# Turning one half batch of q, k and x with crossbar transposes instead of TensorE transposes, and splitting the last output tile, in a fused attention and squared-ReLU kernel

## The chip, the cores and the metric

The kernel runs on one core of a Trainium2 chip. The metric is device time in microseconds (us) per execution; a verdict compares fast runs only, with a 95% interval, and calls a difference real beyond 2%. PE is TensorE, DVE VectorE, ACT ScalarE, POOL GpSimd, SP SyncE; a name with q behind it is that engine's sequencer.

## The reference, cut to what matters

```python
# q, k, v: (4, 8, 768, 64) float32; n_global = 8, n_local = 96
scores = scale * np.matmul(q, k.transpose(0, 1, 3, 2)) + bias     # bias: minus slope of the head x distance
scores = np.where(is_global | is_local, scores, -1e9)             # local window and first 8 keys
a = softmax(scores)
x = np.matmul(a, v)            # -> 3072 tokens x 512
h = np.maximum(x @ w_in, 0.0)  # w_in 512 x 2048
out = (h * h) @ w_out          # w_out 2048 x 512, float32 out
```

The window reaches back less than 128 positions, so each tile of 128 queries needs only its own tile of keys, the one before it, and the 8 global keys.

## The kernel before

The eight "half batches" (384 tokens each, numbered 0 to 7) go through a software pipeline: while TensorE does the two dense layers of one half, it does the attention of the next half in between. To multiply q by k, both must lie with the head dimension on partitions, and the attention result x must be turned too. There are two ways to turn a tile: a TensorE transpose into PSUM followed by a copy, or a DMA "crossbar" transpose from SBUF to SBUF on SP's queue. In the kernel before, halves 0 to 2 use TensorE and halves 3 to 7 the crossbar.

```python
stage_p = ctx.enter_context(tc.tile_pool(name="stage", bufs=2))   # sq, sk: float16 q and k as loaded
...
def list_loads(x):                       # GpSimd's queue: loads that cast float32 to float16
    before = (prev.turned if prev else []) + (halves[x.hb - 1].turned if x.hb > 3 else [])
    ...                                  # plan.load(0.85, emit, before), three each for q, k, v
def turn(x, a):                          # pair a of heads: 6 TensorE transposes into PSUM, 2 copies
    ...
        nc.tensor.transpose(out=trp[:, i, t, :], in_=st[:, t, 2 * a:2 * a + 2, :], identity=ident)
def turn_by_dma(x):                      # one transfer for q and one for k of the half
    ...
        nc.sync.dma_start_transpose(out=x.bt.qk[:, 1 - i, ts]..., in_=getattr(x, name)...)
    for a in range(NPAIR):               # fix_k: DVE copies part of k into kb
        x.qk_ops[a] = x.turned + [plan.add(*fix_k(x, a), x.turned[:1], wait=4.0)]
def to_x(x, a): ...                      # 3 TensorE transposes and a copy
def to_x_by_dma(x, a):
    ...
        nc.sync.dma_start_transpose(out=x.xt[:, a, :]..., in_=st["tm"]...)
...
def attention(x):
    early = x.hb > 2
    for a in range(NPAIR):
        at = 0.04 + 0.16 * a if early else 0.1 + 0.17 * a
        jobs.append((at, lambda a=a: score(x, a)))
        jobs.append((at + 0.17, lambda a=a: attend(x, a)))
        if early:
            jobs.append((at + 0.17, lambda a=a: to_x_by_dma(x, a)))
        else:
            jobs.append((0.04 * a, lambda a=a: turn(x, a)))
            jobs.append((at + 0.3, lambda a=a: to_x(x, a)))
```

Two things matter later. A planner in Python, with estimated durations, chooses the order in which each engine gets its instructions. On the chip an engine can then stand at an instruction whose data is late although others behind it could run (the early loads below show VectorE doing so for 13.92 us). And `stage_p` has two buffers per name, so the loads of half 3 go into the buffers of half 1 and wait on the chip only for half 1, whatever the planner's `before` list says.

The softmax here doesn't subtract the row's maximum and nothing guards it: scores larger than these inputs give would overflow.

Of the kernel before, what the change touches and what calls it, by code (L numbers as in the profile page):

```python
# [8 lines left out]
FP32 = mybir.dt.float32  # L9
# [4 lines left out]
P = 128  # L14
# [130 lines left out]
def kernel(  # L145
# [11 lines left out]
    nc = tc.nc  # L157
# [3 lines left out]
    d_model, d_ff = moe_w_in.shape  # L161
    NT = S // P
    NPAIR = H // 2
    NFT = d_ff // P
    NCT = d_model // P
    HALF = S // 2
    HT = HALF // P
    NHB = 2 * B
# [17 lines left out]
    plan = Plan(1.0, 24.0)  # L186
# [5 lines left out]
    def copy(e, out, in_):  # L192
        if e == "ACT":
            nc.scalar.copy(out=out, in_=in_)  # L194
        else:
            eng(e).tensor_copy(out=out, in_=in_)
# [94 lines left out]
    def list_loads(x):  # L291
        r0 = x.half * HALF
        prev = halves[x.hb - 2] if x.hb >= 2 else None
        before = (prev.turned if prev else []) + (halves[x.hb - 1].turned if x.hb > 3 else [])
        vbefore = [halves[x.hb - x.half - 3].attended[-1]] if x.hb >= 4 else []

        def rows(src, name, t):
            def emit(e):
                dst = (x.bt.v[:, x.half * HT + t, :, 0:D] if name == "v"
                       else staged(x, name)[:, t, :, :])  # L300
                nc.gpsimd.dma_start(out=dst, in_=src[x.b, :, r0 + t * P:r0 + (t + 1) * P, :]  # L301
                                    .rearrange("h p d -> p h d"))
            return plan.load(0.85, emit, vbefore if name == "v" else before)

        if x.half == 0:
            def start(e):
                new_batch(x.bt)
                nc.vector.memset(x.bt.v[:, :, :, D:D + 1], 1.0)
            x.bt.op = plan.add({"DVE": 0.1}, start, vbefore, rank=0)
        if x.hb > 1:  # L310
            x.q_in = [rows(q, "sq", t) for t in range(HT)]
            x.k_in = [rows(k, "sk", t) for t in range(HT)]
            x.v_in = [rows(v, "v", t) for t in range(HT)]
        elif x.hb == 1:
            x.k_in, x.q_in, x.v_in = zip(*((rows(k, "sk", t), rows(q, "sq", t), rows(v, "v", t))
                                           for t in range(HT)))
        else:
            def first(dst, src, eng, e, lag):
                raw = stage_p.tile([P, H, D], FP32, name="r" + dst, tag="r" + dst, bufs=1)
                op = plan.add({e: 0.5}, lambda e: eng.dma_start(  # L320
                    out=raw, in_=src[0, :, 0:P, :].rearrange("h p d -> p h d")), rank=-1)
                op.lag = lag

                def emit(e):
                    copy(e, staged(x, dst)[:, 0], raw)
                return plan.add({"DVE": 0.42, "ACT": 0.54}, emit, [op], rank=0)
            x.k_in = [first("sk", k, nc.scalar, "ACT", 4.1)]
            x.q_in = [first("sq", q, nc.sync, "SP", 3.4)]
            x.v_in = []
            for t in range(1, HT):  # L330
                x.k_in.append(rows(k, "sk", t))
                x.q_in.append(rows(q, "sq", t))
                x.v_in.append(rows(v, "v", t - 1))
            x.v_in.append(rows(v, "v", HT - 1))
        for l in x.v_in:
            l.needs.append(x.bt.op)
        x.bt.v_in = [*getattr(x.bt, "v_in", []), *x.v_in]
# [18 lines left out]
    def fix_v(bt, t0, t1):  # L356
        def emit(e):
            copy(e, bt.vb[:, t0 - 1:t1 - 1], bt.v[:, t0:t1])
            copy(e, bt.vb[0:GR, t0 - 1:t1 - 1], bt.v[0:GR, 0:1].to_broadcast(
                [GR, t1 - t0, H, D + 1]))  # L360
        op = plan.add({"DVE": 0.85}, emit, [bt.v_in[0], *bt.v_in[t0:t1]],
                      wait=0.0 if bt is batches[0] else 4.0)
        for t in range(t0, t1):
            bt.vb_ops[t] = op

    def fix_k(x, a):
        t0, t1 = tiles_before(x)

        def emit(e):
            kt = x.bt.qk[:, 1, :, a, :]  # L370
            copy(e, x.bt.kb[:, a, t0 - 1:t1 - 1, GR:P], kt[:, t0:t1, GR:P])
            copy(e, x.bt.kb[:, a, t0 - 1:t1 - 1, 0:GR],
                 kt[:, 0:1, 0:GR].to_broadcast([P, t1 - t0, GR]))
        return {"DVE": 0.2 + 0.08 * (t1 - t0)}, emit

    def turn(x, a):
        state = {}

        def emit(e):
            state["ps"] = trp = ps_att.tile([P, 2, HT, P], FP16, name="trp", tag="att")  # L380
            warm(trp.rearrange("p i t c -> p (i t c)"))
            for i, st in enumerate((x.sq, x.sk)):
                for t in range(HT):
                    nc.tensor.transpose(out=trp[:, i, t, :], in_=st[:, t, 2 * a:2 * a + 2, :],  # L384
                                        identity=ident)
        job = plan.pe(6 * 0.056, emit, x.q_in + x.k_in + [ident_op], [att])

        def evac(i):
            def emit(e):
                copy(e, x.bt.qk[:, i, x.half * HT:(x.half + 1) * HT, a, :], state["ps"][:, i])  # L390
            return plan.after(job, {"ACT": 0.39, "DVE": 0.31}, emit)
        ops = [evac(0), evac(1)]
        x.turned.append(job)
        x.qk_ops[a] = ops + [plan.add(*fix_k(x, a), [ops[1]])]


    def turn_by_dma(x):
        ts = slice(x.half * HT, (x.half + 1) * HT)
        late = list(halves[x.hb - 2].x_ops.values()) if x.hb > 3 else []
        for i, (name, loads) in enumerate((("sk", x.k_in), ("sq", x.q_in))):  # L400
            def emit(e, i=i, name=name):
                nc.sync.dma_start_transpose(
                    out=x.bt.qk[:, 1 - i, ts].rearrange("p t a c -> p (t a) c"),
                    in_=getattr(x, name).rearrange("p t h d -> p (t h d)"))
            op = plan.add({"SP": 1.7}, emit, [*loads, x.bt.op, *late])
            op.lag = 2.5
            x.turned.append(op)
        for a in range(NPAIR):
            x.qk_ops[a] = x.turned + [plan.add(*fix_k(x, a), x.turned[:1], wait=4.0)]

    GROUPS = {
        0: ([(0, 0), (1, 0), (1, 1)], [(2, 0), (2, 1)]),
# [106 lines left out]
    def to_x_by_dma(x, a):  # L519
        st, norm = x.tm[a]  # L520

        def emit(e):
            if x.xt is None:
                x.xt = h_p.tile([P, NCT, HALF], FP16, name="xt", tag="xt")
            nc.sync.dma_start_transpose(
                out=x.xt[:, a, :].rearrange("p (t c) -> p t c", c=P),
                in_=st["tm"].rearrange("p t e d -> p (t e d)"))
        x.x_ops[a] = plan.add({"SP": 1.2}, emit, [norm])
        x.x_ops[a].lag = 2.5
# [56 lines left out]
    def layer2(x, j, m0):  # L586
# [15 lines left out]
        if m0 + 4 == NFT:  # L602
            def evac(e):
# [4 lines left out]
            plan.add({"SP": 0.6}, lambda e: nc.sync.dma_start(out=out[r0:r0 + P, :], in_=st["y"]),  # L608
                     [y_op])

    for x in halves:
        x.turned, x.attended = [], []
        x.qk_ops, x.phat, x.tm, x.x_ops, x.h2_ops, x.l1, x.l2 = {}, {}, {}, {}, {}, {}, {}
        x.xt = x.h2 = None
# [120 lines left out]

    def attention(x):
        jobs = []
        early = x.hb > 2
        for a in range(NPAIR):
            at = 0.04 + 0.16 * a if early else 0.1 + 0.17 * a  # L740
            jobs.append((at, lambda a=a: score(x, a)))
            jobs.append((at + 0.17, lambda a=a: attend(x, a)))
            if early:
                jobs.append((at + 0.17, lambda a=a: to_x_by_dma(x, a)))
            else:
                jobs.append((0.04 * a, lambda a=a: turn(x, a)))
                jobs.append((at + 0.3, lambda a=a: to_x(x, a)))
        return sorted(jobs, key=lambda j: j[0])

    def merge(main, side):  # L750
# [7 lines left out]
    def l1(x, m0=0):  # L758
        return [lambda m=m: layer1(x, [m]) for m in range(m0, NFT)]

    def l2(x):
        return [lambda j=j, m0=m0: layer2(x, j, m0) for j in range(HT) for m0 in range(0, NFT, 4)]
# [21 lines left out]
    jobs = {}  # L784
# [18 lines left out]
        job()  # L803
    for hb in range(1, NHB):
        x = halves[hb]
        for y in halves[2:4] if hb == 1 else halves[hb + 2:hb + 3]:
            list_loads(y)
        if hb == 1:
            fix_v(halves[2].bt, 1, 2)
        main = l2(x0)[6:] + l2(x) if hb == 1 else l1(x) + l2(x)  # L810
        side = attention(halves[hb + 1]) if hb + 1 < NHB else []
        merge(main, side)
        if hb + 2 < NHB:
            t0, t1 = tiles_before(halves[hb + 2])
            for t in range(t0, t1):
                fix_v(halves[hb + 2].bt, t, t + 1)
            turn_by_dma(halves[hb + 2])
# [37 lines left out]
```

## Time and profile before

| | before |
|---|---|
| time, three runs at first | 222.17 us median (221.47 to 222.4) |
| first trace | 1217.1 us, in a run of 1218.93 us: TensorE was busy for 1211.9 us in it, more than five times as long as in the later trace |
| a later trace at full speed | span 223.6 us, in a slow run: 225.36 us, over 1.5% above the fastest (221.22) of its 20 neighbours (median 222.12) |
| TensorE busy in the later trace | 212.5 us, 95% |

The prediction had only the first trace and shows its lines below. What it could not show is this, from the page of the later trace of the same kernel, taken after the prediction: the clock that TensorE was granted and the load of the DMA engines, in tenths, in 40 slices of 5.6 us.

```profile
span 223.6 us, 4828 instructions
PEclk9999999999999999996999999999999999999999
DMA  9999999999999999999799721157012101220012
```

For the first 23 slices, until about 129 us, the DMA engines are nearly always busy; after that they are mostly idle. This row decides the case. (An ordinary run, that of the tail-only kernel below, shows the same 23 slices.) In the first trace the same bytes were spread over 1217 us (slices of 30 us), so most transfers in it met idle engines:

```profile
DMA  9909000056005002700001000100000000000000
```

And in the later trace TensorE began half 2's first scores, which the changed kernel makes wait, without any idle time before them:

```profile
55.72 0.40 PE L434 MATMUL sp<-qk 64*128 64x128 f16 x8
```

### The profile page before, as it was taken

What the parts mean: (1) busy time and instruction counts of PE and PEld (TensorE: products, weight loads), DVE (VectorE), ACT (ScalarE), POOL (GpSimd) and SP (SyncE); (2) the same over time, 40 slices, a digit from 0 to 9 for tenths busy, and PEclk for the clock granted to TensorE, in tenths of its full rate; (3) what the DMA queues carried; (4) which work ended last, traced back from release to release, by engine and by line L of the source; (5) the groups of instructions that cost most, each with busy time, mean ns of one, the idle gap of its engine ahead of it and who ended that gap; (6) DMA issues with size and microseconds to landing.
All of it is one profiled execution on the core that took longest, in us unless ns stands there. A gap on an engine that the chain in (4) does not pass through costs nothing.

```text
span 1217.1 us, 4828 instructions
## 1 busy us (share of the span) xinstructions
PE 1211.9 (100%) x1912; PEld 457.0 (38%) x1912; DVE 119.1 (10%) x336; ACT 136.9 (11%) x288; POOL 68.6 (6%) x84
## 2 busy tenths in 40 slices
PE   9999999999999999999999999999999999999998
PEld 8765665233333342233322333233322333223322
DVE  2111110001010110001100111001100111000000
ACT  2121101001101110011000110011100211001100
POOL 6203000012001000200000000000000000000000
DMA  9909000056005002700001000100000000000000
GB/s 161 103 0 65 0 1 0 1 56 47 9 22 47 4 6 25 73 9 7 3 12 43 4 3 7 43 9 3 7 12 9 9 6 4 12 17 0 1 9 17
DMA packets 106583, 26.41 MB, mean 22 GB/s; under 512 B 99392, under 2 KB 103488, under 8 KB 106560
## 3 DMA queue, kind: packets, MB, share of 16 engines
q0 software_dynamic: 77024, 13.37, 14.0%
q1 hardware_dynamic: 28496, 12.46, 4.1%
q10 hardware_dynamic: 1040, 0.26, 0.1%
q8 instruction: 15, 0.25, 0.1%
q14 instruction: 8, 0.07, 0.0%
HBM read 27.26 MB, written 6.29 MB: 28 GB/s over the span
## 4 chain that ended last, share of the span: by engine, by line
PE 100%; ACT 0%; DVE 0%; POOL 0%; issue 0%; POOLq 0%
PE yps L593 42%; PE hps L544 42%; PE av L489 4%; PE sp L434 4%; PE trp L210 2%; PE trp L628 1%; PE sp L661 1%; PE av L700 1%; PE sp L654 1%; PE trx L727 1%; PE trp L384 1%; PE sp L207 1%; PE trx L513 0%; PE av L207 0%; PE hps L207 0%; ACT y L194 0%
## 5 line engine op out<-in xcount | busy, mean ns | idle before, releaser
L544 PE MATMUL hps<-xt,w_in_sb 128*128 128x384 f16 (+2 forms) x608 | 517.6, 1215 | 0.0
L593 PE MATMUL yps<-w_out_sb,h 128*128 128x512 f16 x384 | 514.2, 1701 | 0.0
L544 PEld LDWEIGHTS <-w_in_sb 128*128 128x128 f16 x608 | 187.4, 316 | 288.7 <-issue 284.6
L593 PEld LDWEIGHTS <-h 128*128 128x128 f16 x384 | 120.1, 315 | 351.3 <-issue 350.7
L568 ACT ACTIVATE hr<-hps 128x384 f16<-128x384 f32 (+1 forms) x108 | 54.9, 508 | 449.1 <-PE hps L544 422.1
L579 DVE TENSOR_TENSOR h<-hr 128x768 f16<-128x768 f16 (+1 forms) x70 | 36.6, 524 | 566.3 <-ACT hr L568 565.8
L194 ACT COPY y<-yps 128x512 f32<-128x512 f32 x24 | 14.0, 585 | 466.6 <-PE yps L593 466.6
L489 PEld LDWEIGHTS <-phat 128*128 128x128 f16 x264 | 41.7, 220 | 24.5 <-issue 23.1
L489 PE MATMUL av<-v,phat 128*128 128x65 f16 x168 | 44.7, 445 | 0.0
L449 ACT ACTIVATE ex<-sp 128x384 f16<-128x384 f32 x96 | 39.3, 464 | 40.0 <-PE sp L434 38.4
L489 PE MATMUL av<-vb,phat 128*128 128x65 f16 x96 | 36.3, 460 | 0.0
L301 POOL DMA_DIRECT2D sq<-in_q_dram x23 | 20.6, 904 | 219.3 <-DMA qk<-sq 125.9
L434 PE MATMUL sp<-qk 64*128 64x128 f16 x168 | 30.2, 612 | 0.0
L301 POOL DMA_DIRECT2D sk<-in_k_dram x23 | 20.7, 920 | 134.7 <-DMA qk<-sk 133.5
L434 PEld LDWEIGHTS <-qk 64*128 64x128 f16 x168 | 12.3, 175 | 41.4 <-issue 41.2
L301 POOL DMA_DIRECT2D v<-in_v_dram x24 | 21.6, 927 | 90.5 <-DVE rec L496 90.5
L496 DVE RECIPROCAL rec<-av 128x6 f32<-128x6 f32 x24 | 4.7, 196 | 219.0 <-PE av L489 219.0
L434 PE MATMUL sp<-qk,kb 64*128 64x128 f16 x96 | 25.4, 724 | 0.0
L210 PE MATMUL trp<-ident,zero 128*128 128x128 f16 x58 | 20.1, 710 | 1.7 <-DVE ident L233 1.7
L210 PEld LDWEIGHTS <-zero 128*128 128x128 f16 x58 | 16.6, 313 | 3.7 <-DVE zero L769 1.2
L700 PEld LDWEIGHTS <-ph 128*128 128x128 f16 x88 | 15.2, 234 | 3.2 <-issue 2.5
L434 PEld LDWEIGHTS <-kb 64*128 64x128 f16 x96 | 15.8, 329 | 1.3
(65 smaller groups left out, 289.6 us busy)
## 6 DMA issues: line engine op xcount, KB each, us to landing
out_dram<-y SPq DMA_DIRECT2D x24, 256.0 KB, 2.0
v<-in_v_dram POOLq DMA_DIRECT2D x24, 128.0 KB, 4.7
sk<-in_k_dram POOLq DMA_DIRECT2D x23, 128.0 KB, 4.5
sq<-in_q_dram POOLq DMA_DIRECT2D x23, 128.0 KB, 4.3
w_in_sb<-in_moe_w_in_dram POOLq DMA_DIRECT2D x4, 512.0 KB, 8.6
w_out_sb<-in_moe_w_out_dram POOLq DMA_DIRECT2D x4, 512.0 KB, 13.6
xt<-tm SPq DMA_TRANSPOSE x20, 2.3
rsk<-in_k_dram ACTq DMA_DIRECT2D x1, 256.0 KB, 4.7
```

What stands on the lines that cost most here:

```text
L194: nc.scalar.copy(out=out, in_=in_)
L207: nc.tensor.matmul(ps[:, 0:n], lhsT=zero[:, 0:P], rhs=zero[:, 0:n], start=True, stop=True)
L210: nc.tensor.transpose(out=ps[:, 0:n], in_=zero[:, 0:P], identity=ident)
L301: nc.gpsimd.dma_start(out=dst, in_=src[x.b, :, r0 + t * P:r0 + (t + 1) * P, :] .rearrange("h p d -> p h d"))
L434: nc.tensor.matmul(pair[h][:, i * P:(i + 1) * P], lhsT=lhsT, rhs=bt.qk[rows, 0, r, a, :], start=True, stop=True)
L449: nc.scalar.activation(out=st["ex", g][:, h, 0:n], in_=st[g][h][:, 0:n], func=AF.Exp, scale=scale)
L489: nc.tensor.matmul(av[:, h, j, :], lhsT=phat[:, h, c * P:(c + 1) * P], rhs=rhs, start=n == 0, stop=n == len(mine) - 1)
L544: nc.tensor.matmul(st["ps"][:, i * n:(i + 1) * n], lhsT=w_in_sb[:, kk, m * P:(m + 1) * P], rhs=x.xt[:, kk, c0:c1], start=kk == 0, stop=kk ...
L568: nc.scalar.activation(out=o, in_=i, func=AF.Relu)
L579: eng(e).tensor_tensor(out=x.h2[:, m0:m0 + width, c0:c1], in0=hr, in1=hr, op=ALU.mult)
L593: nc.tensor.matmul(st["ps"], lhsT=x.h2[:, m, j * P:(j + 1) * P], rhs=w_out_sb[:, m, :], start=m == 0, stop=m == NFT - 1)
L700: nc.tensor.matmul(av[:, a - a0, h, :], lhsT=st["ph", before][:, h, a, :], rhs=rhs, start=not before, stop=before == kinds[-1])
```

## The change

Its intent: TensorE bounds the kernel, so take 36 transposes of half 2 from it (24 of q and k, 12 of x) and give them to the DMA crossbar; list the loads of half 3 after half 2's transposes; and write the last output tile in two column halves, so that the first is copied and sent under the matmuls of the second.

```diff
-        before = (prev.turned if prev else []) + (halves[x.hb - 1].turned if x.hb > 3 else [])
+        before = (prev.turned if prev else []) + (halves[x.hb - 1].turned if x.hb > 2 else [])
 ... (fix_v, turn_by_dma: shorter waits in the planner for half 2)
+    def last_layer2(x, j):        # the last tile: two groups of 16 matmuls of 256 columns,
+        ...                       # each with its own copy and its own output transfer
     def attention(x):
-        early = x.hb > 2
-            at = 0.04 + 0.16 * a if early else 0.1 + 0.17 * a
+            at = 0.04 + 0.16 * a if x.hb > 2 else 0.05 + 0.14 * a
-            if early:
-                jobs.append((at + 0.17, lambda a=a: to_x_by_dma(x, a)))
-            else:
-                jobs.append((0.04 * a, lambda a=a: turn(x, a)))
-                jobs.append((at + 0.3, lambda a=a: to_x(x, a)))
+            jobs.append((at + 0.17, lambda a=a: to_x_by_dma(x, a)))
 ...
-        for y in halves[2:4] if hb == 1 else halves[hb + 2:hb + 3]:
+        if hb == 1:
+            list_loads(halves[2])
+            turn_by_dma(halves[2])
+            fix_v(halves[2].bt, 1, 2)
+        for y in halves[hb + 2:hb + 3]:
             list_loads(y)
+        if hb == NHB - 1:
+            main = main[:-NFT // 4] + [lambda: last_layer2(x, HT - 1)]
```

More of the change, by code (lines that the diff above doesn't have):

```diff
@@ L361, in fix_v @@
         op = plan.add({"DVE": 0.85}, emit, [bt.v_in[0], *bt.v_in[t0:t1]],
-                      wait=0.0 if bt is batches[0] else 4.0)
+                      wait=0.0 if bt is batches[0] else 0.5 if t1 == 2 and bt is batches[1] else 4.0)
         for t in range(t0, t1):
@@ L404, in emit @@
                     in_=getattr(x, name).rearrange("p t h d -> p (t h d)"))
-            op = plan.add({"SP": 1.7}, emit, [*loads, x.bt.op, *late])
+            op = plan.add({"SP": 1.7}, emit, [*loads, x.bt.op, *late], wait=4.0 if x.hb == 3 else 0.0)
             op.lag = 2.5
@@ L408, in turn_by_dma @@
         for a in range(NPAIR):
-            x.qk_ops[a] = x.turned + [plan.add(*fix_k(x, a), x.turned[:1], wait=4.0)]
+            x.qk_ops[a] = x.turned + [plan.add(*fix_k(x, a), x.turned[:1],
+                                                 wait=4.0 if x.hb > 2 else 0.5)]
     GROUPS = {
@@ L609, in layer2, with emit, evac @@
                      [y_op])
+    def last_layer2(x, j):
+        n = d_model // 2
+        r0 = x.hb * HALF + j * P
+        for c in range(0, d_model, n):
+            st = {}
+            def emit(e, c=c, st=st):
+                st["ps"] = ps_big.tile([P, 512], FP32, name="yps", tag="big")
+                for m in range(NFT):
+                    nc.tensor.matmul(st["ps"][:, 0:n], lhsT=x.h2[:, m, j * P:(j + 1) * P],
+                                     rhs=w_out_sb[:, m, c:c + n], start=m == 0, stop=m == NFT - 1)
+            def evac(e, st=st):
+                st["y"] = y_p.tile([P, d_model], FP32, name="y", tag="y")
+                copy(e, st["y"][:, 0:n], st["ps"][:, 0:n])
+            job = plan.pe(NFT * (n / 2400 + 0.003), emit, [x.h2_ops[m, j] for m in range(NFT)], [big])
+            y_op = plan.after(job, {"ACT": 0.3, "DVE": 0.35}, evac)
+            plan.add({"SP": 0.6}, lambda e, c=c, st=st: nc.sync.dma_start(
+                out=out[r0:r0 + P, c:c + n], in_=st["y"][:, 0:n]), [y_op])
     for x in halves:
@@ L805 @@
         x = halves[hb]
-        for y in halves[2:4] if hb == 1 else halves[hb + 2:hb + 3]:
+        if hb == 1:
[3 more added lines that the diff above has]
+        for y in halves[hb + 2:hb + 3]:
             list_loads(y)
-        if hb == 1:
-            fix_v(halves[2].bt, 1, 2)
         main = l2(x0)[6:] + l2(x) if hb == 1 else l1(x) + l2(x)
+        if hb == NHB - 1:
+            main = main[:-NFT // 4] + [lambda: last_layer2(x, HT - 1)]
         side = attention(halves[hb + 1]) if hb + 1 < NHB else []
```

## The prediction

> **What bounds the kernel now.** I read the times first, then the head of the page, the groups of instructions split by form, the data transfers, three stretches at the start, and the timeline of the last ten microseconds. From the head of the page:
>
> ```profile
> span 1217.1 us, 4828 instructions
> PE 1211.9 (100%) x1912; PEld 457.0 (38%) x1912; DVE 119.1 (10%) x336; ACT 136.9 (11%) x288; POOL 68.6 (6%) x84
> GB/s 161 103 0 65 0 1 0 1 56 47 9 22 47 4 6 25 73 9 7 3 12 43 4 3 7 43 9 3 7 12 9 9 6 4 12 17 0 1 9 17
> PE 100%; ACT 0%; DVE 0%; POOL 0%; issue 0%; POOLq 0%
> ```
>
> The span contradicts the times: three runs took 221.47 to 222.4 us, the profiled one 1217.1. TensorE is busy for 1211.9 us, more than five whole executions. So this trace shows a TensorE far slower than in the timed runs, and every wait of TensorE is hidden in it. The reader should take from it the counts and shapes of TensorE's instructions and the durations of everything else, but no TensorE duration and no absence of a wait. The groups by form:
>
> ```profile
> L593 PE MATMUL yps<-w_out_sb,h 128*128 128x512 f16 x384 | 514.2, 1701 | 0.0
> L544 PE MATMUL hps<-xt,w_in_sb 128*128 128x384 f16 x416 | 419.8, 1372 | 0.0
> ...
> L194 ACT COPY y<-yps 128x512 f32<-128x512 f32 x24 | 14.0, 585 | 466.6 <-PE yps L593 466.6
> ...
> L449 ACT ACTIVATE ex<-sp 128x256 f16<-128x256 f32 x24 | 9.3, 388 | 2.0 <-PE sp L434 0.3
> ...
> L384 PE MATMUL trp<-ident,sq 128*128 128x128 f16 x12 | 5.6, 719 | 0.0
> L384 PE MATMUL trp<-ident,sk 128*128 128x128 f16 x12 | 5.5, 704 | 0.0
> L513 PE MATMUL trx<-ident,tm 128*128 128x128 f16 x12 | 5.4, 675 | 0.0
> ```
>
> The two dense layers are 384 x 512 + 416 x 384 + 96 x 256 + 96 x 128 = 393,216 columns. At one column per cycle of the skill's 2.4 GHz plus 2.5 ns for each of the 992 matmuls that is 166 us. The same rule gives the other 920 matmuls 35 us (the 264 + 88 scores, on half the array's rows, at 0.55 of the rule because two can run side by side: my choice). The stream is about 201 us of the 222: in the timed runs, too, TensorE bounds the kernel, with some 21 us of start, end and waits. Vector and scalar work (119 and 137 us) fits beneath it. What shortens TensorE's stream, the opening or the tail shortens the run; nothing else does.
>
> **What the skill says.** (1) Perfetto Trace Analysis, section "Identifying the Most-Contended Engine": matmul busy time is no measure of the distance to the limit, because matmuls are pipelined. The trace agrees: 100% busy at 5.5 times the timed duration. (2) TensorE: Matmul & The Clock Gate, "Back-to-back issue gap": N/2.4 + 2.5 ns for a warm matmul of N columns, 56 ns for 128 columns, but about 81 ns in a stream of weight load and matmul pairs of 128 columns. The trace's 719 and 1701 ns cannot confirm either; the run's 222 us is compatible with 201 us of stream. (3) DMA: Bandwidth & Descriptors, "Rules for kernel authors": transfers issued from different engines run on the same 16 DMA engines and interleave. So crossbar transposes share them with the loads around them; no run here shows by how much. (4) Same page, "Anatomy of one DMA": a fixed cost of about 2.0 us per transfer, mostly waiting for completion. The trace agrees: 256 KB of output lands in 2.0 us.
>
> **The change part by part.** *Half batch 2.* Removed from TensorE: the 24 transposes of q and k (L384) and the 12 of x (L513). 36 x 56 ns = 2.0 us; at the 81 ns of paired streams 2.9 us; by share of busy time, (5.6 + 5.5 + 5.4) / 1211.9 x 222.17 = 3.0 us. I take 2.3, near the lower value, because the other matmuls around them hide part of a weight load. All of it lies on the path, as TensorE has no slack. The 8 + 4 copies out of PSUM go too (0.48 us each on ACT, 0.36 on DVE, some 5 us), but off the path: worth 0 by themselves. Added: two crossbar transposes for q and k and four for x, on SP's queue.
>
> ```profile
> out_dram<-y SPq DMA_DIRECT2D x24, 256.0 KB, 2.0
> ...
> xt<-tm SPq DMA_TRANSPOSE x20, 2.3
> ...
> qk<-sq SPq DMA_TRANSPOSE x5, 3.9
> qk<-sk SPq DMA_TRANSPOSE x5, 3.9
> ```
>
> They cost TensorE nothing unless it reaches its scores before they land. The program's order shows that TensorE's stream is the same up to the point where half 2's first transposes stood, after 24 output matmuls. In the changed kernel half 2's first scores follow 4 output matmuls later, at 43.6 us of the stream (by the rule above). When are q and k turned?
>
> ```profile
> 0.00:10.00 10.00, 8.33 (x27) 7.50 (x28) 4.54 (x17) 5.07 (x13) 9.25 (x16) 1.00 1.55 135
> 10.00:40.00 30.00, 30.00 (x101) 23.58 (x99) 2.74 (x10) 5.25 (x10) 14.23 (x18) 1.00 1.54 182
> ...
> 5.44 0.43 DVE L196 CAST sk<-rsk 128x512 f16<-128x512 f32 x1
> ```
>
> The first two rows are stretches; their last column is GB/s, 135 in the first 10 us and 182 from 10 to 40. The third is a line of the timeline: start, duration, instruction. Ahead of half 2's q and k stand 6.8 MB as the trace counts them (16 loads of 131 KB, two of 262, eight weight loads of 524). They need 10 + (6.82 - 1.35) / 0.182 = 40 us; the six loads, 0.79 MB, 4.3 more: 44.4. Plus 3.9 for the transpose and about 0.35 for the first copy of k: 48.6 us. TensorE's stream can't do its first real transposes before 5.9 us (end of the second cast above), where the rule puts them at 2.0; so it reaches the scores at 43.6 + 3.9 = 47.5 us without any later wait. But 222.17 - 201 - 3.9 leaves 17 us; some 1.8 lie outside the span (1218.93 for the run against 1217.1) and 3 in the tail, so 12 us are waits and small-tile losses. Most should be in the opening, where short tiles chain from engine to engine; with half of them there TensorE arrives at 53 us, 5 us after the data. I put 0.5 us on the chance of a wait and on new PSUM waits, since the scores, which take four of six banks each, now come slightly closer together (2.5 instead of 3.1 jobs apart).
>
> *The loads of half 3 behind them.* On GpSimd's queue the order of loads is unchanged, and they wait for no crossbar transpose of half 2: the new dependency only steers the planner. So it costs nothing, but these 1.2 MB can meet half 2's transposes.
>
> *Last tile in two column halves.* Today, after the last matmul:
>
> ```profile
> 1207.79 5.81 PE L593 MATMUL yps<-w_out_sb,h 128*128 128x512 f16 x4
> ...
> 1213.64 0.58 ACT L194 COPY y<-yps 128x512 f32<-128x512 f32 x1 [20.58 <-PE yps L593]
> 1214.25 0.33 SPq L608 DMA_DIRECT2D out_dram<-y  x1
> ```
>
> Afterwards the first half is copied and written under the second half's 16 matmuls. What remains is a copy of 256 columns, 388 ns by the ACT row of that width instead of 585: 0.2 us. The transfer is 128 KB instead of 256; most of its 2.0 us is fixed, so I take 0.3 off. Sixteen more matmuls cost 16 x 2.5 ns = 0.04. Sum: 0.45 us gained.
>
> Total: -2.3 - 0.45 + 0.5 = -2.25 us, or 219.9 from 222.17 (1.0%).
>
> **The rivals.** *The turn takes the gain back.* TensorE stalls at half 2's first scores because the transposes land late. For it: 47.5 against 48.6 us above if the opening has no waits, and loads of v and of half 3 running beside them. If the transposes take twice 3.9 us, the scores wait up to 4 us longer. Against it: the 12 us of waits not accounted for. It would give 221 to 224. *The gain is larger.* The transposes stood in a chain (transpose, copy out, copy of k, scores) through two PSUM buffers; if TensorE waited there, up to 2 us more go: 217 to 218. The trace cannot speak for it, since the slow TensorE hides such waits; against it, 1.2 us of output matmuls stand between neighbouring links. *SP's queue holds back x.* The crossbar transposes of x for pairs 1 and 2 stand behind half 3's transpose of k, which waits for its loads. Those follow half 2's loads directly and land by about 52 us; x is wanted when 60.7 us of stream are done. Against it, then; if it happens, 1 to 3 us are lost.
>
> **Range and chances.** Removed work between 2.0 and 3.0, tail 0.2 to 0.7, new waits 0 to 2: the change lies between -3.7 and -0.2, and the runs before spread by 0.9 us. So 218.4 to 221.9. Over 2% faster means below 217.7, which needs an unseen chain to go: 6%. Over 2% slower means above 226.6, a stall beyond anything estimated: 3%. Within 2%: 91%.
>
> **What would show it.** Right: 1892 matmuls in TensorE's row (36 fewer, 16 more), no transposes of half 2 left in the groups, six crossbar transposes each of q and of k and 24 of x among the transfers; at the end a copy near 0.39 us in place of 0.58. A stall would show as idle time of TensorE before half 2's first scores, ended by a transfer or by DVE's copy of k, or before half 2's first layer, ended by a transpose of x; if the trace is of a slow TensorE again, it can show neither, and the landing times of half 2's transposes must serve. I would be wrong if these land far above 3.9 us and the time is 222 or more, or if the time is below 217.7: then TensorE waited for something that this trace hides.

## The result, and the profile after

| | before | changed |
|---|---|---|
| median | 222.28 us (221.47 to 222.55, 4 runs) | 232.06 us (229.17 to 233.67, 4 runs) |
| ratio of fast runs | | 1.0368 [1.0268, 1.0467]: slower |

Ratios here and below are the mean time of one kernel's fast runs over that of the other's fast runs of the same rounds, so they are not quite the ratio of the medians. Two of the changed kernel's four runs (233.67 and 232.65 us) were labelled slow, being over 1.5% above its fastest. The profiled run was the fastest, 229.17 us.

The page of the changed kernel, at full speed this time, to be held against the rows above:

```profile
span 227.4 us, 4799 instructions
...
PE 211.7 (93%) x1892; PEld 126.3 (56%) x1892; DVE 116.6 (51%) x333; ACT 123.9 (54%) x280; POOL 68.5 (30%) x84
...
PEclk9999999999589999999999999999999999999999
DMA  9999999999999999999799660129011200211012
...
PE 67%; DMA 25%; POOL 5%; DVE 1%; issue 1%; ACT 0%; SPq 0%; POOLq 0%
```

There are 1892 matmuls, as intended. But TensorE is busy for 93% of a longer span, its clock falls in slices 11 and 12 (57 to 68 us), and DMA has 25% of the chain that ended last (the last row). The timeline of TensorE shows where; the columns are start, duration, instruction, and in brackets the idle time before it with what ended it:

```profile
52.81 0.38 PE L594 MATMUL yps<-w_out_sb,h 128*128 128x512 f16 x1
59.55 0.61 PE L435 MATMUL sp<-qk 64*128 64x128 f16 x8 [6.36 <-DMA qk<-sk]
60.20 4.92 PE L594 MATMUL yps<-w_out_sb,h 128*128 128x512 f16 x12
...
81.26 0.32 PE L545 MATMUL hps<-xt,w_in_sb 128*128 128x384 f16 x1 [1.04 <-DMA xt<-tm]
82.71 0.97 PE L545 MATMUL hps<-xt,w_in_sb 128*128 128x384 f16 x5 [1.13 <-DMA xt<-tm]
```

TensorE is done with its other work at 52.81 + 0.38 = 53.2 us and then stands for 6.36 us, until the transpose of half 2's k has landed. The next twelve matmuls of 512 columns take 4.92 us, where twelve take 2.76 at full clock (below). A second pair of waits, 2.2 us in all, comes before half 2's first dense layer, for the transposed x. Stretches of 2 us of the same trace; the third figure from the end is the granted clock:

```profile
54.00:56.00 2.00, 0.00 (x0) 0.00 (x0) 0.00 (x0) 0.00 (x0) 0.87 (x1) 1.00 1.71 67
...
60.00:62.00 2.00, 2.00 (x11) 0.70 (x6) 0.84 (x7) 1.43 (x4) 0.97 (x2) 0.50 2.41 158
...
64.00:66.00 2.00, 2.00 (x26) 1.03 (x25) 0.05 (x1) 0.57 (x2) 1.79 (x4) 0.85 2.42 158
```

The clock is halved towards the end of the wait and comes back only about 5 us after work resumes. Last, the transfers issued from 40 to 50 us, with size and median time from issue to landing, and then the issue of the two transposes on SP's queue:

```profile
sq<-in_q_dram POOLq DMA_DIRECT2D x3, 128.0 KB, 10.6
sk<-in_k_dram POOLq DMA_DIRECT2D x3, 128.0 KB, 13.9
qk<-sq SPq DMA_TRANSPOSE x1, 10.4
qk<-sk SPq DMA_TRANSPOSE x1, 13.2
```

```profile
43.66 2.34 SPq L402 DMA_TRANSPOSE qk<-sq  x1
46.33 5.03 SPq L402 DMA_TRANSPOSE qk<-sk  x1
```

The transpose of k, issued at 46.33, lands 13.2 us later, at 59.5; that ends the wait. Beside it run half 3's loads of q, k and v, which GpSimd issued between 43.1 and 51.6 us.

How large is the loss as a sum? The tail-only kernel below has the old turns and a trace of an ordinary run (222.31 us, span 220.5, one wait of 1.05 us for x). Against it the changed kernel has 6.36 + 2.17 - 1.05 = 7.5 us more waiting and 4.92 - 2.76 + 0.61 - 0.40 = 2.4 us at half clock, and 36 transposes less (2.0 us): 7.9. The spans differ by 227.4 - 220.5 = 6.9, so the three items account for the loss to within about a microsecond. (The openings differ too: the tail-only trace has one wait of 2.4 us there, the changed kernel's several short ones.) The other runs of the changed kernel are 2.3 to 4.5 us longer; the turn-only trace below shows such a run, with longer waits of the same two kinds.

### The profile page after: what moved, and what is told of

The parts are those of the page before. It is cut to its first block, busy times and chain, and to the rows that moved or that the text cites. A ratio compares the mean times of both kernels' runs of the same rounds, so it can differ in the third digit from the quotient of the medians.

```text
span 227.4 us, 4799 instructions
## 1 busy us (share of the span) xinstructions
PE 211.7 (93%) x1892; PEld 126.3 (56%) x1892; DVE 116.6 (51%) x333; ACT 123.9 (54%) x280; POOL 68.5 (30%) x84
## 3 DMA queue, kind: packets, MB, share of 16 engines
q0 software_dynamic: 77024, 13.37, 83.2%
## 4 chain that ended last, share of the span: by engine, by line
PE 67%; DMA 25%; POOL 5%; DVE 1%; issue 1%; ACT 0%; SPq 0%; POOLq 0%
PE yps L594 29%; PE hps L545 28%; DMA qk<-sk 8%; DMA w_out_sb<-in_moe_w_out_dram 6%; DMA sk<-in_k_dram 5%; PE sp L435 4%; DMA w_in_sb<-in_moe_w_in_dram 4%; PE av L490 4%; DMA xt<-tm 2%; POOL v L301 2%; PE yps L622 2%; POOL sq L301 1%; POOL w_in_sb L342 1%; POOL sk L301 1%; DVE phat L462 0%
## 5 line engine op out<-in xcount | busy, mean ns | idle before, releaser
L545 PE MATMUL hps<-xt,w_in_sb 128*128 128x384 f16 (+2 forms) x608 | 89.6, 301 | 2.9 <-DMA xt<-tm 2.2
L594 PE MATMUL yps<-w_out_sb,h 128*128 128x512 f16 x368 | 84.5, 386 | 0.0
L545 PEld LDWEIGHTS <-w_in_sb 128*128 128x128 f16 x608 | 53.7, 98 | 30.0 <-issue 2.6
L594 PEld LDWEIGHTS <-h 128*128 128x128 f16 x368 | 35.8, 99 | 42.0 <-issue 3.0
L194 ACT COPY y<-yps 128x512 f32<-128x512 f32 (+1 forms) x24 | 13.6, 567 | 63.7 <-PE yps L594 61.2
L435 PE MATMUL sp<-qk 64*128 64x128 f16 x168 | 9.1, 223 | 6.4 <-DMA qk<-sk 6.4
L499 DVE TENSOR_TENSOR tm<-av,rec 128x384 f16<-128x384 f32 x24 | 13.4, 557 | 0.9
L497 DVE RECIPROCAL rec<-av 128x6 f32<-128x6 f32 x24 | 4.7, 197 | 15.6 <-PE av L490 15.3
L490 PEld LDWEIGHTS <-phat 128*128 128x128 f16 x264 | 9.9, 98 | 3.4
L490 PE MATMUL av<-v,phat 128*128 128x65 f16 x168 | 11.4, 194 | 0.0
L490 PE MATMUL av<-vb,phat 128*128 128x65 f16 x96 | 10.2, 194 | 0.0
```

What stands on the lines that cost most here:

```text
L194: nc.scalar.copy(out=out, in_=in_)
L435: nc.tensor.matmul(pair[h][:, i * P:(i + 1) * P], lhsT=lhsT, rhs=bt.qk[rows, 0, r, a, :], start=True, stop=True)
L490: nc.tensor.matmul(av[:, h, j, :], lhsT=phat[:, h, c * P:(c + 1) * P], rhs=rhs, start=n == 0, stop=n == len(mine) - 1)
L499: nc.vector.tensor_tensor(out=st["tm"].rearrange("p t e d -> p e t d"), in0=av[:, :, :, 0:D], in1=rec[:, :, :, None].to_broadcast([P, 2, H ...
L545: nc.tensor.matmul(st["ps"][:, i * n:(i + 1) * n], lhsT=w_in_sb[:, kk, m * P:(m + 1) * P], rhs=x.xt[:, kk, c0:c1], start=kk == 0, stop=kk ...
L594: nc.tensor.matmul(st["ps"], lhsT=x.h2[:, m, j * P:(j + 1) * P], rhs=w_out_sb[:, m, :], start=m == 0, stop=m == NFT - 1)
```

## The experiments

Theory A, formed from these traces: in the first 130 us the DMA engines are saturated, a crossbar transpose shares them with the casting loads, and so it lands late; TensorE, which now depends on it, waits and then loses its clock. Rival B: these transposes are slow by themselves, loads or not. Rival C (the recorded expectations call it H): they are late because SP's queue issues in order, and what stands ahead of them takes time.

All fourteen kernels were correct. "Before" in each set is the kernel before, run on the same chip in the same rounds.

### The kernel before again, at full speed

No edit; a look.

> The kernel before, unchanged, for a trace at TensorE's full speed, which the first trace of it was not. Both theories: about 222.2 us. Theory A (the crossbar transposes of half 2 were stretched by the loads of half 3 that are in flight with them): half 3's crossbar transposes of q and k are slow here too, since half 4's loads flow beside them, but they are not awaited: TensorE idles under 0.5 us between 45 and 85 us and its clock stays at 1.0 there. Rival B (a crossbar transpose of q or k simply takes over 10 us at this place, whatever runs beside it): the same here, it can't be told apart by this run.

One run, 225.36 us (recorded as state unknown, a slow run by its neighbours). Its trace gave the rows shown under "Time and profile before". It also has the disease in a small form: half 3's q and k, turned by the crossbar among the loads, took 6.6 and 5.7 us to land, but had 20 us to do so; half 3's x did not, and TensorE waited 2.61 us for it at about 100 us, after which its clock was halved for a few microseconds (in the tail-only trace, an ordinary run, the wait is 1.05 us and the clock stays). The experiment on half 3's x below shows these lines.

### The two parts apart: tail only, and turn only

```diff
 # tail only: the kernel before, plus last_layer2 and
+        if hb == NHB - 1:
+            main = main[:-NFT // 4] + [lambda: last_layer2(x, HT - 1)]
 # turn only: the changed kernel, without these two lines
```

> The kernel before with the last output tile in two column halves and nothing else. The prediction's term: 0.45 us less than before, a ratio of 0.998. If the tail costs something (more matmuls, two transfers instead of one): 1.000 or more. Neither A nor B bears on it.

> The changed kernel with the last output tile in one piece: half 2's crossbar transposes alone. A and B both: the whole loss is here, about 9 to 10 us over before (ratio 1.035 to 1.05), with TensorE idle some 6 us before half 2's first scores, at half clock for some 5 us after it, and idle 2 us more before half 2's first layer. If the tail were part of the loss, the ratio would be under 1.03.

Tail only: 222.10 us (220.42 to 223.36, 14 runs), ratio 0.9996 [0.997, 1.0023]. Turn only: 233.62 us (233.52 to 234.55, 4 runs), ratio 1.0516 [1.0465, 1.0567]. So the turn is the whole loss. The tail's copy fell from 0.59 to 0.37 us and its transfer from 2.0 to 1.7, as predicted, but a gain of 0.45 us (0.2%) is inside the interval and stays unresolved. The turn-only trace has the waits of the changed kernel, longer: 7.22 us for k, then 1.99 and 1.36 us for x.

### Each half of the turn alone: q and k, and x

```diff
 # q and k alone: the changed kernel, half 2's x back on TensorE
-            jobs.append((at + 0.17, lambda a=a: to_x_by_dma(x, a)))
+            if x.hb > 2: jobs.append((at + 0.17, lambda a=a: to_x_by_dma(x, a)))
+            else:        jobs.append((at + 0.3, lambda a=a: to_x(x, a)))
 # x alone: the kernel before, half 2's x by crossbar
-                jobs.append((at + 0.3, lambda a=a: to_x(x, a)))
+                jobs.append((at + 0.17, lambda a=a: to_x_by_dma(x, a)))
```

> The changed kernel with half 2's x turned on TensorE again: the crossbar turns its q and k alone, half 3's loads not gated. A: the first wait (6 to 8 us, and half clock for some 5 us after it) is all there, the second wait is gone; 227.5 to 230.5 us, that is 2 us or more less than the 231 to 233 of the whole change. If q and k were not the main cost: under 225.

> The kernel before with half 2's x turned by the crossbar, q and k on TensorE as before: removes 12 transposes from TensorE (0.7 us by 56 ns each). A: the four transposes of x share the DMA engines with half 3's crossbar transposes and half 4's loads, land in 7 to 10 us instead of 2.3, and TensorE waits for the last of them before half 2's first layer by 0 to 4 us: 221.5 to 226. H: x stands before half 3's transposes on SP's queue here (the program's order shows it), so no wait at all: 221 to 222.

q and k alone: 228.27 us (226.73 to 229.71), ratio 1.0267 [1.0199, 1.0335]. x alone: 226.96 us (226.66 to 228.65), ratio 1.0235 [1.0169, 1.0301]. Four runs each; both intervals reach just under 2%, so both verdicts are "unclear" at that line, but both are clearly above 1. Together, 2.7 + 2.4 = 5.1%, they add up to the 5.2% of the turn-only kernel, within their intervals. The time of x alone is just above the range that theory A expected, and far above the 221 to 222 us of the rival. With q and k alone TensorE waits 6.26 us at the scores, as in the changed kernel. With x alone, the summary of the x tiles and a line of TensorE's timeline:

```profile
DMA to landing us min/median/max: 3.5/7.0/7.6
```

```profile
77.83 1.06 PE L544 MATMUL hps<-xt,w_in_sb 128*128 128x384 f16 x5 [3.19 <-DMA xt<-tm]
```

The transposes of x land in 7.0 us (median) here. Each was issued within 0.1 us of the end of its producer on DVE (the last at 70.94, after 70.91), so nothing was held back on SP's queue. So rival C is not needed for a wait: slow landing alone makes one. But in the changed kernel C is at work too: x's last pair was ready at 75.5 us and issued at 78.31, behind half 3's k and the other x transposes. The end of its producer on DVE, and two issues on SP's queue:

```profile
74.98 0.56 DVE L499 TENSOR_TENSOR tm<-av,rec 128x384 f16<-128x384 f32 x1
```

```profile
72.48 2.35 SPq L402 DMA_TRANSPOSE qk<-sk  x1
...
78.31 1.26 SPq L526 DMA_TRANSPOSE xt<-tm  x1
```

It landed 4.4 us after its issue. Issued at 75.5, it would by that duration have landed at 79.9, before TensorE first stood still for x at 80.2; the pair before it (ready at 72.7, issued at 76.22, landed 5.0 us later) likewise. By this estimate, which no run tests, the holding back on SP's queue carries most of the 2.2 us of this second wait of the changed kernel.

### The loads of half 3 held back on the chip

```diff
 # staged(), changed kernel: half 3 loads into half 2's staging tile, so it must wait for half 2's transposes
         if getattr(x, name, None) is None:
+            if x.hb == 3:                  # second variant: x.hb >= 3, and halves[x.hb - 1]
+                setattr(x, name, getattr(halves[2], name))
+                return getattr(x, name)
```

> The changed kernel, but half 3's q and k are loaded into half 2's staging buffers, so that the chip itself makes each of these loads wait until half 2's crossbar transpose of that buffer has landed. A: q's transpose lands in 4 to 7 us and k's by 53 us (only v's three loads still run beside them), TensorE waits at most 1 us before half 2's first scores, the clock stays at 1.0, and the time is 219.5 to 222 us (a second wait of 2 us before half 2's first layer may stay). B: k's transpose still takes over 10 us, TensorE idles 5 us or more, and the time stays at 229 us or more.

> The changed kernel with one staging buffer for q and one for k from half 2 on, so that every half's loads of q and k wait on the chip for the crossbar transposes of the half before. The gate on half 3 alone took the first wait away (0.34 us left) and brought a second of 9.4 us before half 2's first layer. Theory A (crossbar transposes are slow whenever loads flow beside them): now half 4's loads no longer run beside half 3's transposes and half 2's transposes of x; q's, k's and x's land in 3 to 7 us each, both waits together are under 2 us, the clock stays at 1.0, and the time is 219.5 to 222.5 us. Rival H (the second wait comes from the order on SP's queue, x behind half 3's k, whatever the loads do): over 5 us of waiting before half 2's first layer stay, and the time is 226 us or more.

Half 3 only: 232.16 us (231.71 to 232.51), ratio 1.044 [1.039, 1.049]. All halves from 3: 228.76 us (228.11 to 229.65), ratio 1.0293 [1.0242, 1.0344]. As a cure, a miss. As a test of the cause, the first is the sharpest of the study. TensorE's timeline with half 3 held back, and the transfers issued from 45 to 50 us:

```profile
53.51 0.40 PE L438 MATMUL sp<-qk 64*128 64x128 f16 x8 [0.34 <-DMA qk<-sk]
...
54.21 2.76 PE L597 MATMUL yps<-w_out_sb,h 128*128 128x512 f16 x12
...
79.58 0.48 PE L548 MATMUL hps<-xt,w_in_sb 128*128 128x384 f16 x1 [7.09 <-DMA xt<-tm]
```

```profile
qk<-sk SPq DMA_TRANSPOSE x1, 7.0
```

Only half 3's loads were moved, and k's transpose lands in 7.0 us instead of 13.2; the wait at the scores falls from 6.36 to 0.34 us, and the twelve matmuls after it run at full clock. Rival B fell here: the same transpose is twice as fast without its neighbours. But half 3's loads, with half 4's behind them, now run where half 2's x is turned: x lands in 9.1 us (median), and TensorE waits 7.09 + 0.92 + 1.34 = 9.4 us for it. The wait was moved, not removed. Here C has a large part: x's last pair was ready at 68.0 us and issued at 74.50, 6.5 us later, behind half 3's k on SP's queue.

With all later halves held back, 4.79 us remain before half 2's layer, with the last x transpose ready at 71.2 us, issued at 74.0 and landing 6.8 us later, and 1.12 us at the scores. The expectation had put the line between theory A and the rival at 226 us and at 5 us of waiting for x: the time is on the rival's side, the wait just short of it. For x the two causes are not separated by this run.

### Dummy matmuls in the wait

```diff
 # score(), changed kernel: 24 matmuls of 512 columns on zeros before half 2's first scores
+                    if x.hb == 2 and a == 0:
+                        for _ in range(24):
+                            nc.tensor.matmul(pair[0], lhsT=zero[:, 0:P], rhs=zero, start=True, stop=True)
```

This asks whether the lost clock is a cost of its own.

> The changed kernel with 24 matmuls on zeros, 512 columns each, just before half 2's first scores, in the time in which TensorE would wait (24 x 216 ns = 5.2 us of a wait of 6 to 8). If the granted clock falls to one half because of the wait: the clock stays at 1.0 (or falls for under 1 us), and the 12 output matmuls after the first scores take 2.6 us, not 4.9: 2 to 2.5 us less than the change's 231 to 232, so 228.5 to 230. If the clock falls for another reason: no less than the changed kernel.

234.58 us (233.26 to 235.3, 4 runs), ratio 1.0545 [1.0489, 1.0602]: a miss in time. TensorE's timeline:

```profile
60.06 2.76 PE L598 MATMUL yps<-w_out_sb,h 128*128 128x512 f16 x12
...
85.34 1.76 PE L549 MATMUL hps<-xt,w_in_sb 128*128 128x384 f16 x5 [5.32 <-DMA xt<-tm]
```

The twelve matmuls after the scores take 2.76 us instead of 4.92, so idling is what halves the clock, and filling prevents it. But the next wait, for x, grew from 2.2 to 1.64 + 5.32 us and the clock was lost there. In this stretch the end is set by the transfers, and time won on TensorE before them is waited away: x's last pair was ready 2.3 us earlier than in the changed kernel (73.2 us), but SP's queue issued it at 78.97 instead of 78.31. Why it then took 6.3 us to land instead of 4.4 stays open.

### The loads of half 4 fenced off from half 2's x

```diff
 # the x-alone kernel: a tiny GpSimd write to half 2's last x tile, ahead of half 4's loads on the same
 # queue; it can't run before the crossbar has read that tile
+        if hb == 2:
+            plan.load(0.0, lambda e: nc.gpsimd.memset(
+                halves[2].tm[NPAIR - 1][0]["tm"][:, 0, 0, 0:1], 0.0), [x.x_ops[NPAIR - 1]])
```

> The kernel before with half 2's x turned by the crossbar (as in the run of x alone, 226.96 us with 4.5 us of waits before half 2's first layer), and a fence on GpSimd's queue: half 4's loads, and all loads behind them, wait until the last of the four transposes of x has landed. A: x's transposes now have the DMA engines nearly to themselves, land in 2.3 to 4 us instead of 7, the wait before half 2's first layer is under 1 us and the clock stays at 1.0: 221.2 to 223 us (a later wait for half 4 is possible, since its loads start some 14 us later). H (order on SP's queue or the crossbar's own latency): the wait stays at 3 us or more, 225 to 228.

229.60 us (227.94 to 230.83, 4 runs), ratio 1.0342 [1.0291, 1.0393]: a miss in time, and no better than x alone without the fence. As a test of the cause it worked. The summary of half 2's x tiles, and a line of TensorE's timeline:

```profile
DMA to landing us min/median/max: 2.3/2.3/3.7
```

```profile
105.29 1.76 PE L544 MATMUL hps<-xt,w_in_sb 128*128 128x384 f16 x5 [4.50 <-DMA xt<-tm]
```

With the loads out of the way, x lands in 2.3 us instead of 7.0: the very number that the prediction took from the slow trace. TensorE does not wait before half 2's layer. The delayed loads then met half 3's x instead: 1.91 and 4.50 us of waiting there, at 100 and 105 us, and half clock after them.

### Half 2's q and k loaded before the second weights

If q and k arrived and were turned early, TensorE would not wait for them. One kernel loads them ahead of `w_out` (x on TensorE); the other keeps x on the crossbar and adds the fence above.

```diff
 # both from the changed kernel; list_loads gets an argument that selects q and k, or v
     list_w_in((2, 3))
+    list_loads(halves[2], "qk")
     list_w_out()
...
-            list_loads(halves[2])
+            list_loads(halves[2], "v")
```

> The changed kernel with half 2's q and k loaded ahead of the w_out weights instead of behind them, and half 2's x on TensorE again: the crossbar turns only q and k, some 10 us earlier. A (TensorE waited because the transposes ended late in a stretch of full DMA engines, not because a transpose by crossbar costs it anything): they may still take 8 to 13 us each beside the weights, but land by 48 us, before TensorE comes to half 2's scores at 53; no wait, no half clock, and the 24 transposes are gained: 220.3 to 222 us, ratio 0.991 to 0.999. If w_out, now 4.3 us later, is late instead: a wait before the first output matmuls at 47 us, and 222 to 226.

> The whole change with both remedies: half 2's q and k loaded ahead of w_out, and half 4's loads fenced behind half 2's transposes of x. A: both waits are gone or under 1 us together, no half clock before 85 us, and the gain that the prediction counted on comes out: 219.8 to 221.5 us, ratio 0.989 to 0.997. If waits appear further on, with half 4's loads late: 222 to 225.

Early loads: 230.84 us (229.68 to 231.93, 6 runs), ratio 1.0401 [1.0365, 1.0438]. Early and fenced: 238.34 us (236.1 to 240.14, 6 runs), ratio 1.0719 [1.0673, 1.0765]. Both misses. In the first, the two transposes now ran beside the weight loads and took 15.3 us each. The timelines of DVE, ACT and TensorE, one line of each:

```profile
55.02 0.62 DVE L196 COPY kb<-qk 128x96 f16<-128x96 f16 x6 [13.92 <-DMA qk<-sk]
```

```profile
56.07 2.40 ACT L572 ACTIVATE hr<-hps 128x384 f16<-128x384 f32 x6 [11.45 <-DVE h L583]
```

```profile
56.61 8.76 PE L597 MATMUL yps<-w_out_sb,h 128*128 128x512 f16 x28 [8.62 <-ACT hr L572]
```

Read from the top: DVE had its copies of k next in its order, ahead of squares for the dense layer, and stood 13.92 us for the transpose; ACT, out of buffers, waited for DVE; TensorE waited for ACT. A late transfer thus stopped an engine that had other work behind it. For the second kernel the profiled run was a slow one, and shows TensorE idle for 9.65 us before output matmuls; it was not followed further.

### Half 3's x back on TensorE

The reverse of the change, on the kernel before: if theory A holds, half 3's x too is better off on TensorE.

```diff
 # attention(), the kernel before
+            if x.hb == 3:
+                jobs.append((at + 0.3, lambda a=a: to_x(x, a)))
+            elif early:
-            if early:
                 jobs.append((at + 0.17, lambda a=a: to_x_by_dma(x, a)))
```

> The opposite step: the kernel before with half 3's x taken from the crossbar back to TensorE (12 transposes more). Two traces of the kernel before, or nearly so, show TensorE waiting 1.1 and 2.6 us for a crossbar transpose of x before half 3's first layer, and a fall of the clock around it. A (crossbar transposes that TensorE soon needs lose while loads fill the DMA engines): 0.7 us of TensorE work is added, the wait and the clock loss go (1.1 to 2.6 and about 1.5): 219.5 to 221.7 us, ratio 0.988 to 0.997. If only TensorE's count of instructions decides: 0.7 us more than before, ratio 1.003.

221.38 us (220.84 to 223.2, 22 runs) against 222.23 (59 runs), ratio 0.9964 [0.9946, 0.9982]. Two lines of the kernel before at full speed, a line of TensorE's timeline and the stretch from 84 to 108 us (its columns: length, then busy time of PE, PEld, DVE, ACT, POOL, the clock, DMA, GB/s):

```profile
101.29 1.56 PE L544 MATMUL hps<-xt,w_in_sb 128*128 128x384 f16 x5 [2.61 <-DMA xt<-tm]
```

```profile
84.00:108.00 24.00, 21.39 (x157) 10.96 (x156) 10.37 (x27) 9.85 (x25) 8.49 (x10) 0.93 1.77 147
```

the same stretch of the tail-only kernel, an ordinary run with the same turns,

```profile
84.00:108.00 24.00, 22.95 (x179) 12.16 (x179) 12.99 (x36) 12.44 (x31) 7.96 (x9) 1.00 1.77 136
```

and that of the kernel with half 3's x on TensorE:

```profile
84.00:108.00 24.00, 24.00 (x205) 13.27 (x203) 14.60 (x44) 13.21 (x33) 9.00 (x11) 1.00 1.63 140
```

TensorE is busy for all 24 us, at full clock, instead of 22.95 (21.39 at 0.93 in the slow run). In the whole trace no wait of TensorE for a DMA transpose is left. It does twelve transposes more than before, and it is faster: by only 0.4%, under the 2% line, but with an interval clear of 1. This is the fastest version of the study. (In an ordinary run the wait is only 1.05 us, which is why so little was to be had.)

### Loads held back and x on TensorE

```diff
 # changed kernel, staged() as in the second variant above (halves from 3 on), and
 # half 2's x on TensorE; in the second kernel also half 3's
-            jobs.append((at + 0.17, lambda a=a: to_x_by_dma(x, a)))
+            if x.hb > 2: ...to_x_by_dma       # second kernel: x.hb > 3
+            else:        jobs.append((at + 0.3, lambda a=a: to_x(x, a)))
```

> The changed kernel with half 2's q and k by crossbar, x on TensorE, and every half's loads of q and k made to wait for the half before's crossbar transposes. A: the first wait is 0.3 to 1.5 us as in the two gated runs, none before half 2's first layer, so the 24 transposes (1.3 us) just about pay for it: 220.5 to 223 us, ratio 0.993 to 1.004. If q and k by crossbar cost something beside their lateness: over 225.

> The run before this one with half 3's x on TensorE as well. A: as that run, minus a wait of 0 to 2.6 us before half 3's first layer, plus 0.7 us of transposes: 219.5 to 222.5 us. If it is no faster than the run before this one, half 3's x isn't waited for there.

222.32 us (220.21 to 229.62, 22 runs), ratio 0.9985 [0.9962, 1.0008], and 222.36 us (220.24 to 225.76, 22 runs), ratio 0.9983 [0.9955, 1.0011]. In the first trace q and k land in 7.1 us and TensorE has no wait at the scores. The first of these kernels is the q-and-k-alone kernel plus the held-back loads, and nothing else: its ratio went from 1.0267 to 0.9985. So the crossbar turn of q and k stops costing anything once the loads beside it wait, which is theory A's clearest test in time, but the 1.3 us of its 24 removed transposes (0.7 for the second kernel, which removes twelve on balance) do not arrive in the time either. Where they went was not found: the first trace shows 1.35 us before half 3's layer, the second (a run labelled slow) 1.25 us at the scores and 2.78 us before a transpose of x.

## Why the prediction was wrong

- **The bound: right.** At full speed TensorE is 95% busy in the kernel before.
- **What is removed: right.** 1892 matmuls are left. In the full-speed trace a group of three transposes starts every 0.165 us, 55 ns each, so 36 are 2.0 us: the lower of the values that the prediction weighed, not its 2.3. Its choice for the scores fits too: in the changed kernel's trace they start in pairs, one pair every 56 ns.
- **TensorE's arrival at half 2's scores, 53 us: right.** Measured 53.2.
- **Half 2's loads, 44.4 us: off by 2.** The last part of k landed near 46.3, when its transpose was issued.
- **The step that failed: "Plus 3.9 for the transpose and about 0.35 for the first copy of k: 48.6 us."** The transpose took 13.2 us, so TensorE, predicted to arrive "5 us after the data", arrived 6.4 us before it. The 3.9 was a median of transposes in a trace whose TensorE was more than five times too slow, and whose DMA engines were therefore mostly idle. The prediction had seen that this trace was useless for TensorE's durations, but called "the durations of everything else" safe; a transfer's duration depends on what runs beside it, so it was not. That trace even held a hint: its first transpose of q, at 108.5 us, the one of q and k that was issued among the loads, took 6.6 us, the others 3.7 to 4.4.
- **"So it costs nothing" (half 3's loads behind them): wrong.** The prediction saw correctly that the new dependency only steers the planner and that these loads meet half 2's transposes, and gave it no price. Holding just these loads back took k's landing from 13.2 to 7.0 us and the wait from 6.36 to 0.34.
- **Not in the sum at all: the clock.** After 6.4 us of idling TensorE ran at half clock for about 5 us more, 2.4 us lost. The dummy matmuls show that it follows from the idling.
- **"SP's queue holds back x", argued against: it happened.** Its 1 to 3 us were lost (2.2), with x's last pair issued 2.8 us after it was ready. But the queue did not stand waiting for half 3's loads, as the prediction feared: from 68.1 to 80.2 us it issued one transfer after the other, 3.57 and 2.35 us of that for half 3's q and k. And without any holding back x can be late too: x alone, issued at once, made TensorE wait 4.5 us, since it landed in 7.0 us instead of 2.3.
- **"The turn takes the gain back": the right mechanism, a size too small.** It allowed twice 3.9 us, a wait of up to 4 us and 221 to 224. The transpose took more than three times 3.9, and x and the clock were added.
- **The tail: unresolved.** Its parts measured as predicted; its 0.45 us is inside the interval.

What stays open: how much of the 7.0 us that q and k still take with half 3 held back is due to loads of v and outputs, how the late x divides between slow landing and SP's queue in the whole change, and why the kernels with everything held back do not gain the removed work.

## What to carry to other kernels

Before moving work from a busy engine to the DMA engines, look at the row of DMA load in the very stretch where it will run, at full speed: a duration measured among idle engines says nothing about a saturated stretch. Here moving work off the bounding engine lost 4%, and moving twelve transposes back to it gained 0.4%. And holding the competing loads back tends to move the wait to the next transfer, as long as the same bytes must pass in the same stretch. One thing that the pages show was not tried: in the later trace of the kernel before, GpSimd's queue moved its 13.37 MB in 77,024 packets, some 174 bytes each, which took 87.2% of the 16 engines' span, while the queue of the transposes and outputs moved 12.46 MB in 28,496 packets and 26.2%. Whether loads in larger packets would free the engines is not shown.

## What the Trainium skill lacked or had wrong

- DMA: Bandwidth & Descriptors, section "Latency and other measured facts", gives a DMA transpose an effective bandwidth of 261 GB/s, or about 350 to 400 when contiguous, with no word on traffic beside it. Here a transpose of k moves 128 x 1536 float16 values, 393 KB: 13.2 us is 30 GB/s, and 7.0 us 56, both beside casting loads; one of x went from 2.3 us (loads fenced off) to 7.0. A warning that transposes beside loads in a saturated stretch can take three times as long might have changed this prediction.
- TensorE: Matmul & The Clock Gate, section "Back-to-back issue gap", calls about 131 ns per matmul the sustained figure for 512 columns and says that N/2.4 + 2.5 over-counts there. In the changed kernel 32 such matmuls with their weight loads took 6.91 us in a full stretch, 216 ns each: the formula holds and 131 does not.
- TensorE: Matmul & The Clock Gate, section "Seeing it yourself", warns that the recorded clock events can be unreliable, and tells of a clock stuck at a quarter for over 50 us. The first trace here goes beyond that: 1217.1 us, where other executions of the kernel took 222, with a mean granted clock of 1.000. Perfetto Trace Analysis has no advice to compare a trace's span with the timed runs before using any duration in it, those of transfers included.
